# Linear-attention and feed-forward on one core: interleaving the two stages, folding w3 @ w_out, and keeping activations on chip

## The chip, the cores and the metric

One core of one Trainium2 chip runs the whole program. The time is device microseconds of one execution (us). Six parts of the core matter here: PE (TensorE, matrix products and transposes; PEld is its weight load), DVE (VectorE), ACT (ScalarE), POOL (GpSimd, which also issues the converting DMAs of this kernel), SP (SyncE, which issues the other DMAs), and the 16 DMA engines that all queues share. A line number such as L184 is a line of the kernel before.

## The reference, cut to what matters

```python
batch, n_heads, seq, head_dim = (4, 8, 768, 48)        # S = 768, D = 48
for t in range(S):                                      # attention with a decayed state
    kt, vt, rt, wt = (k[:, :, t], v[:, :, t], r[:, :, t], w[:, :, t])
    cur = np.einsum('bhd,bhe->bhde', u[None] * kt, vt)
    y[:, :, t] = np.einsum('bhd,bhde->bhe', rt, state + cur)
    state = wt[:, :, :, None] * state + np.einsum('bhd,bhe->bhde', kt, vt)
x = y.transpose(0, 2, 1, 3).reshape(B * S, H * D)       # 3072 tokens x 384
a = x @ w1                                              # 384 x 1024
b = x @ w2                                              # 384 x 1024
h = a * b @ w3                                          # 1024 x 1024
out = h @ w_out                                         # 1024 x 384, float32
```

There is nothing between `@ w3` and `@ w_out`, so `(a * b) @ (w3 @ w_out)` gives the same output up to rounding.

## The kernel before, in words

The kernel is written in a tile framework: the program names tiles, pools and operations, and the framework puts the instructions of each engine in an order at build time and adds the waits. Each engine then works through its own list in that fixed order. A pool with `bufs=2` gives two buffers in turn; an allocation waits until the oldest buffer is read for the last time.

The work has two stages, one after the other.

Attention treats a batch's 768 steps as 6 chunks of 128. One chunk of one batch is called a unit here; there are 24. Batches go in pairs (`BG = 2`). For each batch r, k and v arrive through POOL's queue (converted to bf16, 0.59 MB each, 6144 rows of 96 bytes) and w through SP's. ACT takes the logarithm of w (L119); per chunk two products with triangular matrices (L129, L132) give running sums, ACT their exponentials, DVE the scaled k and r (L131, L134), and 8 one-column products the decay of the whole chunk (L136). DVE computes the diagonal term for a whole batch at once (L143 to L149). Then each unit runs: 8 transposes of the scaled k and 8 of r, one per head (L166, L170), each set followed by a copy out of PSUM on ACT (L167, L171); 8 products with the state (L178); 8 products between chunk positions (L184), masked on DVE (L186); 8 products with v (L191); the addition of the diagonal (L195); a store of y to DRAM; 8 products that make the state's update (L202), and the update (L206 to L208).

The feed-forward stage reads y back from DRAM with three transposing DMAs (L216) and works on 6 blocks of 512 tokens. Per block: 8 times 3+3 products of 128x128 by 512 columns for a and b (L225, L228), a copy on ACT (L232) and a product on DVE (L233); 64 products of 512 columns with w3 (L239) and 8 copies (L242); 4 times 8 products of 384 columns with w_out (L247), a copy and a store.

The four weight matrices are loaded through POOL's queue, written ahead of r, k and v. Kt_bf, Rt_bf, csp, ktrps, rtrps, Mps, Yps, KVps and y_c in the rows below are tiles of this attention part; a_ps, b_ps, abT, h_ps, hT and o_ps those of the feed-forward.

Of the kernel before, what the change touches and what calls it, by code (L numbers as in the profile page):

```python
# [7 lines left out]
F32 = mybir.dt.float32  # L8
BF = mybir.dt.bfloat16
Alu = mybir.AluOpType  # L10
# [4 lines left out]
def kernel(  # L15
# [12 lines left out]
):  # L28
    nc = tc.nc

    B, H, S, D = r.shape
    C = 128
    NC = S // C
    HC = H * NC
    DM = H * D
    NTOK = B * S
    DFF = moe_w3.shape[0]
    DP = 128

    P = 128  # L40
# [3 lines left out]
    NT = NTOK // TB  # L44

    dram = ctx.enter_context(tc.tile_pool(name="dram", bufs=1, space=bass.MemoryType.DRAM))
    y_dram = dram.tile([NTOK, DM], BF)
    kt_dram = dram.tile([C, HC * DP], BF)
    rt_dram = dram.tile([C, HC * DP], BF)
# [8 lines left out]
    LT_strict = consts.tile([C, C], BF)  # L58
# [4 lines left out]
    mask_tiled = consts.tile([C, H, C], BF)  # L63
    nc.gpsimd.memset(mask_tiled, 1.0)
    nc.gpsimd.affine_select(mask_tiled, mask_tiled, compare_op=Alu.is_gt, fill=0.0,
                            base=0, channel_multiplier=-1, pattern=[[0, H], [1, C]])

    ones_c = consts.tile([C, 1], BF)
    nc.gpsimd.memset(ones_c, 1.0)

    I128 = consts.tile([C, C], BF)
    nc.gpsimd.memset(I128, 0.0)
    nc.gpsimd.affine_select(I128, I128, compare_op=Alu.not_equal, fill=1.0,
                            base=0, channel_multiplier=1, pattern=[[-1, C]])

    u_bc = consts.tile([C, H, D], F32)
    nc.sync.dma_start(u_bc, u.partition_broadcast(C))

    wpool = ctx.enter_context(tc.tile_pool(name="moe_w", bufs=1))
# [3 lines left out]
    wo_bf = wpool.tile([P, FI, DM], BF)  # L83
    nc.gpsimd.dma_start(w1_bf, moe_w1.rearrange("(di dp) f -> dp di f", dp=P))
# [4 lines left out]
    BG = 2  # L89

    with tc.tile_pool(name="attn_io", bufs=2) as sbio, \
         tc.tile_pool(name="attn_sbuf", bufs=BG) as sb, \
         tc.tile_pool(name="attn_sbuf1", bufs=1) as sb1, \
         tc.tile_pool(name="attn_psum", bufs=1, space=bass.MemoryType.PSUM) as ps:

        for bg in range(B // BG):
            st = {}
            for b in range(bg * BG, bg * BG + BG):
                S0_f32 = sb.tile([D, H, D], F32, tag="S0_f")
                S0_bf = sb.tile([D, H, D], BF, tag="S0_b")  # L100
                Kt_bf = sb.tile([C, HC, D], BF, tag="Kt")
                Rt_bf = sb.tile([C, HC, D], BF, tag="Rt")
                Kt4 = Kt_bf.rearrange("t (h c) d -> t h c d", h=H)
                Rt4 = Rt_bf.rearrange("t (h c) d -> t h c d", h=H)

                def rearr(ap):
                    return ap[b].rearrange("h (c t) d -> t (h c) d", t=C)

                r_bf = sbio.tile([C, HC, D], BF, tag="rin")
                k_bf = sbio.tile([C, HC, D], BF, tag="kin")  # L110
                v_bf = sbio.tile([C, HC, D], BF, tag="vin")
                w_f = sbio.tile([C, HC, D], F32, tag="win")
# [12 lines left out]
                r4 = r_bf.rearrange("t (h c) d -> t h c d", h=H)
                pclog_ps = ps.tile([D, HC], F32, tag="pclog", bufs=1)
                for c in range(NC):
                    csp = ps.tile([C, H * D], F32, tag="cs", bufs=1)
                    nc.tensor.matmul(csp, lhsT=LT_incl, rhs=lw4[:, :, c, :], start=True, stop=True)  # L129
                    nc.scalar.activation(NEt, csp, Act.Exp, scale=-1.0)  # L130
                    nc.vector.tensor_mul(Kt4[:, :, c, :], k4[:, :, c, :], NEt)  # L131
                    nc.tensor.matmul(csp, lhsT=LT_strict, rhs=lw4[:, :, c, :], start=True, stop=True)  # L132
                    nc.scalar.activation(Et, csp, Act.Exp)
                    nc.vector.tensor_mul(Rt4[:, :, c, :], r4[:, :, c, :], Et)  # L134
                    for h in range(H):
                        nc.tensor.matmul(pclog_ps[:, h * NC + c:h * NC + c + 1], lhsT=lw4[:, h, c, :],  # L136
                                         rhs=ones_c, start=(c == 0 and h == 0), stop=(c == NC - 1 and h == H - 1))
                pc_all = sb.tile([D, HC], F32, tag="pc_all")
                nc.scalar.activation(pc_all, pclog_ps, Act.Exp)

                uk = sb.tile([C, HC, D], F32, tag="uk")
                d_all = sb.tile([C, HC], F32, tag="d_all")
                nc.vector.tensor_mul(  # L143
                    uk.rearrange("t (h c) d -> t h c d", h=H), k4,
                    u_bc[:, :, None, :].to_broadcast([C, H, NC, D]))
                nc.vector.tensor_mul(uk, uk, r_bf)  # L146
                nc.vector.reduce_sum(d_all, uk, axis=mybir.AxisListType.X)  # L147
                y_diag = sb.tile([C, HC, D], BF, tag="y_diag")
                nc.vector.tensor_mul(y_diag, v_bf, d_all[:, :, None].to_broadcast([C, HC, D]))  # L149

                nc.vector.memset(S0_f32, 0.0)
                nc.vector.memset(S0_bf, 0.0)

                st[b] = dict(S0_f32=S0_f32, S0_bf=S0_bf, Kt4=Kt4, Rt4=Rt4,
                             v4=v_bf.rearrange("t (h c) d -> t h c d", h=H),
                             yd4=y_diag.rearrange("t (h c) d -> t h c d", h=H),
                             pc4=pc_all.rearrange("d (h c) -> d h c", h=H))

            for c in range(NC):
                for b in range(bg * BG, bg * BG + BG):  # L160
                    bs = st[b]
# [12 lines left out]

                    Mbf = sb.tile([C, H, C], BF, tag="M_bf")
                    Yps = ps.tile([C, H * D], F32, tag="Y_ps", bufs=1)
                    for h in range(H):
                        nc.tensor.matmul(Yps[:, h * D:(h + 1) * D], lhsT=RtT[:, h, :],  # L178
                                         rhs=bs["S0_bf"][:, h, :], start=(h == 0), stop=False)
                    for g in range(2):  # L180
                        Mps = ps.tile([C, (H // 2) * C], F32, tag=f"M_ps{g}", bufs=1)
                        for hi in range(H // 2):
                            h = g * (H // 2) + hi
                            nc.tensor.matmul(Mps[:, hi * C:(hi + 1) * C], lhsT=KtT[:, h, :],  # L184
                                             rhs=RtT[:, h, :], start=(hi == 0), stop=(hi == H // 2 - 1))
                        nc.vector.tensor_mul(Mbf[:, g * (H // 2):(g + 1) * (H // 2), :],  # L186
# [23 lines left out]
    with tc.tile_pool(name="moe_sbuf", bufs=2) as msb, \  # L210
# [4 lines left out]
        for di in range(DI):  # L215
            nc.sync.dma_start_transpose(xT[:, di, :], y_dram[:, di * P:(di + 1) * P])  # L216
# [66 lines left out]
```

## Time and profile before

| | us |
|---|---|
| median of 2 runs (419.14 to 419.93) | 419.53 |
| span of the profiled execution, first to last instruction | 417.6 |
| so around the span, by the median | 1.9 |
| PE busy / weight load busy in the span | 315.4 / 177.6 |
| DVE / ACT / POOL busy in the span | 175.6 / 154.9 / 33.4 |

The span is that of one execution under the profiler; the times are of executions without it. Busy time is the sum over instructions of an engine. A PE that is called busy may still be running at half its clock, which the profile gives as the granted clock (1.0 is 2.4 GHz, 0.5 is 1.2 GHz).

### The profile page before, as it was taken

To read this page: it belongs to the slowest core of one execution; us is meant where nothing else is said; L and a number is where in the kernel's file an instruction comes from. 1 tells how busy PE (TensorE), PEld (TensorE's weight loads), DVE (VectorE), ACT (ScalarE), POOL (GpSimd) and SP (SyncE) were. 2 spreads that over 40 slices of the span, in tenths; PEclk is the share of its full clock that TensorE was granted. 3 is DMA by queue.
4 is the path that set the end of the run, shared out by engine and by line. 5 is a ranking of instruction groups with operands and counts; after the bars stand their busy time and mean duration, and the time that the engine had idled before them with its cause. 6 is when DMAs were issued, how large, how long until landed. Compare 5 with 4: busy or idle time off the path is not lost.

```text
span 417.6 us, 5433 instructions
## 1 busy us (share of the span) xinstructions
PE 315.4 (76%) x2256; PEld 177.6 (43%) x2256; DVE 175.6 (42%) x264; ACT 154.9 (37%) x232; POOL 33.4 (8%) x29
## 2 busy tenths in 40 slices
PE   0301034677999747399992699999999999999996
PEld 0201021445777614177771244544544445445443
DVE  1000069795656899975573140330420411402502
ACT  1503033777465336345540133243232332331431
POOL 9100043412000400000000000000000000000000
PEclk9999999985555555655555599999999999999999
DMA  8999999979300980000004700200200201101002
GB/s 157 225 227 215 164 108 129 90 49 111 44 19 26 93 44 2 0 30 21 20 28 98 149 0 2 75 0 2 76 2 0 76 2 38 39 0 57 21 0 75
DMA packets 99400, 26.23 MB, mean 63 GB/s; under 512 B 84144, under 2 KB 97584, under 8 KB 99376
## 3 DMA queue, kind: packets, MB, share of 16 engines
q0 software_dynamic: 76800, 11.54, 40.4%
q1 hardware_dynamic: 22576, 14.36, 13.7%
q8 instruction: 17, 0.28, 0.3%
q14 instruction: 7, 0.06, 0.0%
HBM read 27.98 MB, written 7.08 MB: 84 GB/s over the span
## 4 chain that ended last, share of the span: by engine, by line
PE 63%; DVE 12%; issue 12%; ACT 4%; DMA 4%; POOL 3%; SPq 2%; ACTq 0%; POOLq 0%
PE h_ps L239 20%; PE a_ps L225 8%; PE o_ps L247 7%; PE b_ps L228 7%; PE Mps L184 5%; PE ktrps L166 4%; PE rtrps L170 4%; PE Yps L191 3%; DVE y_diag L149 2%; DMA v_bf<-in_v_dram 2%; DVE d_all L147 2%; DVE uk L146 2%; SPq L216 2%; PE Yps L178 2%; DVE Rt_bf L134 1%
## 5 line engine op out<-in xcount | busy, mean ns | idle before, releaser
L239 PE MATMUL h_ps<-abT,w_bf 128*128 128x512 bf16 x384 | 83.9, 379 | 0.0
L225 PE MATMUL a_ps<-xT,w_bf 128*128 128x512 bf16 x144 | 56.4, 396 | 11.7 <-DMA xT<-y_dram 11.7
L239 PEld LDWEIGHTS <-w_bf 128*128 128x128 bf16 x384 | 37.6, 98 | 45.3
L228 PE MATMUL b_ps<-xT,w_bf 128*128 128x512 bf16 x144 | 56.0, 393 | 0.0
L232 ACT COPY a_sb<-a_ps 128x512 f32<-128x512 f32 x48 | 28.1, 586 | 73.6 <-PE a_ps L225 72.2
L251 DVE COPY o_sb<-o_ps 128x384 f32<-128x384 f32 x24 | 13.4, 557 | 97.5 <-PE o_ps L247 97.5
L233 DVE TENSOR_TENSOR abT<-a_sb,b_ps 128x512 bf16<-128x512 f32 x48 | 33.0, 688 | 47.8 <-ACT a_sb L232 45.9
L242 ACT CAST hT<-h_ps 128x512 bf16<-128x512 f32 x48 | 28.1, 586 | 56.0 <-PE h_ps L239 56.0
L166 PE MATMUL ktrps<-I,Kt_bf 128*48 128x128 bf16 x192 | 30.3, 300 | 23.2 <-DVE Kt_bf L131 22.8
L167 ACT COPY trsb<-ktrps 48x1024 bf16<-48x1024 bf16 x24 | 24.1, 1005 | 38.4 <-PE Yps L178 36.9
L134 DVE TENSOR_TENSOR Rt_bf<-r_bf,Et 128x384 bf16<-128x384 bf16 x24 | 13.1, 546 | 54.9 <-DMA r_bf<-in_r_dram 50.8
L166 PEld LDWEIGHTS <-Kt_bf 128*48 128x48 bf16 x192 | 18.0, 139 | 33.9 <-DVE Kt_bf L131 23.0
L247 PE MATMUL o_ps<-wo_bf,hT 128*128 128x384 bf16 x192 | 32.2, 326 | 0.0
L186 DVE TENSOR_TENSOR Mbf<-Mps,mask_tiled 128x512 bf16<-128x512 f32 x48 | 30.7, 675 | 0.0
L170 PE MATMUL rtrps<-I,Rt_bf 128*48 128x128 bf16 x192 | 28.4, 304 | 2.3 <-ACT trsb L171 1.3
L129 PE MATMUL csp<-lw_bf,LT_incl 128*128 128x384 bf16 x24 | 11.0, 460 | 23.3 <-ACT lw_bf L119 12.8
L184 PE MATMUL Mps<-trsb 48*128 48x128 bf16 x192 | 28.6, 303 | 0.0
L195 DVE TENSOR_TENSOR y_c<-Yps,y_diag 128x384 bf16<-128x384 f32 x24 | 13.4, 557 | 31.2 <-PE Yps L191 31.2
L225 PEld LDWEIGHTS <-w_bf 128*128 128x128 bf16 x144 | 14.6, 101 | 27.6 <-issue 12.1
L171 ACT COPY trsb<-rtrps 48x1024 bf16<-48x1024 bf16 x24 | 24.1, 1005 | 2.1 <-PE rtrps L170 2.1
L130 ACT ACTIVATE NEt<-csp 128x384 f32<-128x384 f32 x24 | 11.7, 489 | 35.0 <-DVE Kt_bf L131 29.0
L247 PEld LDWEIGHTS <-hT 128*128 128x128 bf16 x192 | 18.8, 98 | 13.1
(51 smaller groups left out, 313.8 us busy)
## 6 DMA issues: line engine op xcount, KB each, us to landing
out_dram<-o_sb SPq DMA_DIRECT2D x24, 192.0 KB, 1.9
r_bf<-in_r_dram POOLq DMA_DIRECT2D x4, 576.0 KB, 10.5
k_bf<-in_k_dram POOLq DMA_DIRECT2D x4, 576.0 KB, 8.8
v_bf<-in_v_dram POOLq DMA_DIRECT2D x4, 576.0 KB, 8.5
y_dram<-y_c SPq DMA_DIRECT2D x24, 96.0 KB, 1.6
w_bf<-in_moe_w_dram POOLq DMA_DIRECT2D x1, 2048.0 KB, 26.2
w_bf<-in_moe_w_dram POOLq DMA_DIRECT2D x2, 768.0 KB, 12.3
wo_bf<-in_moe_w_out_dram POOLq DMA_DIRECT2D x1, 768.0 KB, 32.2
```

The lines of the kernel that those rows point to most:

```text
L166: nc.tensor.transpose(ktrps[:, h, :], Kt4[:, h, c, :], I128)
L167: nc.scalar.copy(trsb[:, 0], ktrps)
L170: nc.tensor.transpose(rtrps[:, h, :], Rt4[:, h, c, :], I128)
L184: nc.tensor.matmul(Mps[:, hi * C:(hi + 1) * C], lhsT=KtT[:, h, :], rhs=RtT[:, h, :], start=(hi == 0), stop=(hi == H // 2 - 1))
L186: nc.vector.tensor_mul(Mbf[:, g * (H // 2):(g + 1) * (H // 2), :], Mps.rearrange("s (h t) -> s h t", h=H // 2), mask_tiled[:, :(H // 2), :])
L225: nc.tensor.matmul(a_ps, lhsT=w1_bf[:, di, fi * P:(fi + 1) * P], rhs=xT[:, di, tb * TB:(tb + 1) * TB], start=(di == 0), stop=(di == DI - 1))
L228: nc.tensor.matmul(b_ps, lhsT=w2_bf[:, di, fi * P:(fi + 1) * P], rhs=xT[:, di, tb * TB:(tb + 1) * TB], start=(di == 0), stop=(di == DI - 1))
L232: nc.scalar.copy(a_sb, a_ps)
L233: nc.vector.tensor_mul(abT[:, fi, :], a_sb, b_ps)
L239: nc.tensor.matmul(h_ps, lhsT=w3_bf[:, fi, gi * P:(gi + 1) * P], rhs=abT[:, fi, :], start=(fi == 0), stop=(fi == FI - 1))
L242: nc.scalar.copy(hT[:, gi, :], h_ps)
L247: nc.tensor.matmul(o_ps, lhsT=hT[:, gi, ts * P:(ts + 1) * P], rhs=wo_bf[:, gi, :], start=(gi == 0), stop=(gi == FI - 1))
```

## The change

- w3 @ w_out is computed once on the chip: 64 transposes of 128x128 blocks of w3, then 8 times 8 products of 384 columns into `w34`. Per block the 64 products with w3 are gone; the out products take `abT` and `w34`.
- Two heads share the partitions: scaled k and r lie in tiles padded from 48 to 64 columns a head, so one transpose turns two heads (8 a unit instead of 16, one ACT copy of 128x1024 instead of two of 48x1024). The products between positions take head pairs from partitions 0 to 47 and 64 to 111; the state's update writes two heads to the two halves of PSUM's partitions; the product with the state is one per pair with a block-diagonal state.
- y is transposed on PE (3 a unit) and copied by ACT straight into the feed-forward's input; the DRAM round trip is gone.
- Inputs are loaded per half batch (3 chunks, a group), one DMA per chunk and tensor, the first two groups ahead of the weights. Later groups are written at the first unit of the group two before them.
- The diagonal term is computed per unit, with its three products on POOL; POOL also makes the block-diagonal state (two products a unit).
- The program is written in this order: units 0 to 3, then for each block a quarter of its feed-forward work after each unit of the next block. Blocks 0 to 4 have four units beside them, block 5 none; block 0 also has the w3 @ w_out work.

The core of the new code (the removed lines are those printed above):

```diff
+    ps_ffn = ctx.enter_context(tc.tile_pool(name="ps_ffn", bufs=3, space=bass.MemoryType.PSUM))
+    ps_att = ctx.enter_context(tc.tile_pool(name="ps_att", bufs=2, space=bass.MemoryType.PSUM))
+    ps_m = ctx.enter_context(tc.tile_pool(name="ps_m", bufs=2, space=bass.MemoryType.PSUM))
+    ps_y = ctx.enter_context(tc.tile_pool(name="ps_y", bufs=1, space=bass.MemoryType.PSUM))
...
+    def load_group(b, g):
+        kr_in = inp.tile([C, G, 2, H, D], BF, tag="kr_in")
+        v_in = inp.tile([C, G, H, D], BF, tag="v_in")
+        w_in = inp.tile([C, G, H, D], F32, tag="w_in", bufs=2)
+        for i in range(G):
+            nc.sync.dma_start(w_in[:, i], src(w, b, g)[:, i])
+        for i in range(G):
+            nc.gpsimd.dma_start(kr_in[:, i, 0], src(k, b, g)[:, i])
+            nc.gpsimd.dma_start(kr_in[:, i, 1], src(r, b, g)[:, i])
+        for i in range(G):
+            nc.gpsimd.dma_start(v_in[:, i], src(v, b, g)[:, i])
...
+    def prep_group(b, g):
...
+        for i in range(G):
+            nc.scalar.activation(lw[:, i, :, 0:D], w_in[:, i], Act.Ln)
...
+    def att_a(n):
...
+        for j, (lt, sc) in enumerate(((LT_incl, -1.0), (LT_strict, 1.0))):
+            cs = ps_att.tile([C, H, D], F32, tag="att")
+            nc.tensor.matmul(cs, lhsT=lt, rhs=lw[:, i, :, 0:D], start=True, stop=True)
+            nc.scalar.activation(e_sb[:, j], cs, Act.Exp, scale=sc)
+        krt = kr_st[n % NS]
+        for j in range(2):
+            nc.vector.tensor_mul(krt[:, j, :, 0:D], kr_in[:, i, j], e_sb[:, j])
+        tr = ps_att.tile([C, 2, HP, C], BF, tag="att")
+        for j in range(2):
+            for p in range(HP):
+                nc.tensor.transpose(tr[:, j, p, :],
+                                    krt[:, j, 2 * p:2 * p + 2, :].rearrange("t h d -> t (h d)"), I128)
+        trs = work.tile([C, 2, HP, C], BF, tag="trs")
+        nc.scalar.copy(trs, tr)
+        uk = work.tile([C, H, D], F32, tag="uk")
+        nc.gpsimd.tensor_mul(uk, kr_in[:, i, 0], u_bc)
+        nc.gpsimd.tensor_mul(uk, uk, kr_in[:, i, 1])
+        dsum = work.tile([C, H], F32, tag="dsum")
+        nc.vector.reduce_sum(dsum, uk, axis=mybir.AxisListType.X)
+        yd = work.tile([C, H, D], BF, tag="yd")
+        nc.gpsimd.tensor_mul(yd, v_in[:, i], dsum[:, :, None].to_broadcast([C, H, D]))
...
+    def att_b(n):
...
+        for p in range(HP):
+            for q in range(2):
+                o = q * DP
+                nc.tensor.matmul(mps[q][:, p, :], lhsT=trs[o:o + D, 0, p, :],
+                                 rhs=trs[o:o + D, 1, p, :], start=True, stop=True)
+        for q in range(2):
+            nc.vector.tensor_mul(mbf[:, q], mps[q], mask)
+        if c < NC - 1:
+            kv = ps_att.tile([C, HP, D + 1], F32, tag="att")
+            for p in range(HP):
+                for q in range(2):
+                    nc.tensor.matmul(kv[q * DP:(q + 1) * DP, p, 0:D],
+                                     lhsT=krt[:, 0, 2 * p + q, :], rhs=v_in[:, i, 2 * p + q, :],
+                                     start=True, stop=True)
+                nc.tensor.matmul(kv[:, p, D:D + 1],
+                                 lhsT=lw[:, i, 2 * p:2 * p + 2, :].rearrange("t h d -> t (h d)"),
+                                 rhs=ones_c, start=True, stop=True)
+            nc.scalar.activation(pc[:, :, None], kv[:, :, D:D + 1], Act.Exp)
...
+                nc.vector.tensor_add(ts_, prev[b][0], kv[:, :, 0:D])
...
+            for q in range(2):
+                o = q * DP
+                nc.gpsimd.tensor_mul(s_bd[o:o + DP, :, q * D:(q + 1) * D], ts_[o:o + DP],
+                                     pc[o:o + DP, :, None].to_broadcast([DP, HP, D]))
...
+                nc.vector.tensor_mul(s_f, ts_, pc[:, :, None].to_broadcast([C, HP, D]))
...
+        nc.vector.tensor_add(y_bf.rearrange("t (h e) -> t h e", h=H), y, yd)
+        yt = ps_att.tile([C, DI, C], BF, tag="att")
+        for di in range(DI):
+            nc.tensor.transpose(yt[:, di, :], y_bf[:, di * P:(di + 1) * P], I128)
...
+        nc.scalar.copy(xts[j][:, :, qd * C:(qd + 1) * C], yt)
...
+    def ffn_out(j, t):
+        o_ps = ps_ffn.tile([P, DM], F32, tag="f", name="o_ps")
+        for fi in range(FI):
+            nc.tensor.matmul(o_ps, lhsT=abts[j][:, fi, t * P:(t + 1) * P], rhs=w34[:, fi, :],
+                             start=(fi == 0), stop=(fi == FI - 1))
+        nc.scalar.copy(o_sb, o_ps)
...
+    load_group(0, 0)
...
+    load_group(0, 1)
     nc.gpsimd.dma_start(w1_bf, moe_w1.rearrange("(di dp) f -> dp di f", dp=P))
...
+    def att(n):
+        b, c = divmod(n, NC)
+        if c % G == 0:
+            nxt = b * NG + c // G + 2
+            if nxt < B * NG:
+                load_group(nxt // NG, nxt % NG)
+            prep_group(b, c // G)
+        att_a(n)
+        att_b(n)
...
+    for n in range(UPB):
+        att(n)
+    for j in range(NB):
+        parts = [lambda fi=fi: ffn_ab(j, fi) for fi in range(FI)]
+        if j == 0:
+            parts += fill
+        parts += [lambda t=t: ffn_out(j, t) for t in range(UPB)]
+        units = [n for n in range((j + 1) * UPB, (j + 2) * UPB) if n < NU]
+        k_ = 0
+        for q in range(UPB):
+            if q < len(units):
+                att(units[q])
+            e = len(parts) * (q + 1) // UPB
+            while k_ < e:
+                parts[k_]()
+                k_ += 1
```

`ffn_ab` is the a/b loop of before with both tiles from `ps_ffn`; `fill` is the list of the 8 w3 transpose steps and the 8 product steps into `w34`.

## Rows read from the trace of the kernel before

**Rows 1.** The page: busy us of each engine over the whole span

```profile
PE 315.4 (76%) x2256; PEld 177.6 (43%) x2256; DVE 175.6 (42%) x264; ACT 154.9 (37%) x232; POOL 33.4 (8%) x29
```

**Rows 2.** The page: the span in 40 slices, granted TensorE clock in tenths

```profile
PEclk9999999985555555655555599999999999999999
```

**Rows 3.** Windows: busy us (instructions) of PE, PEld, DVE, ACT, POOL; granted clock, DMA share, GB/s

```profile
100.00:120.00 20.00, 20.00 (x214) 14.77 (x214) 12.11 (x23) 10.74 (x15) 0.00 (x0) 0.50 0.66 56
...
260.00:300.00 40.00, 40.00 (x203) 19.66 (x202) 10.91 (x18) 11.72 (x20) 0.00 (x0) 1.00 0.11 40
```

**Rows 4.** Chain of work that ended last, in order of time: start us, us, what

```profile
109.53 0.43 PE Yps L178 x8
...
111.00 0.54 PE Mps L184 x4
111.54 0.66 PE ktrps L166 x5
...
222.10 0.54 DVE y_c L195
...
231.98 5.45 DMA xT<-y_dram
...
248.32 13.81 PE h_ps L239 x64
262.13 5.20 PE o_ps L247 x32
```

**Rows 5.** Timeline of PE: start us, us, engine, line, operation, tiles, count

```profile
157.18 0.48 PE L132 MATMUL csp<-lw_bf,LT_strict 128*128 128x384 bf16 x1 [1.87 <-ACT NEt L130]
...
165.07 0.85 PE L170 MATMUL rtrps<-I,Rt_bf 128*48 128x128 bf16 x6
...
168.22 0.34 PE L129 MATMUL csp<-lw_bf,LT_incl 128*128 128x384 bf16 x1
```

**Rows 6.** Timeline of the start, all engines

```profile
12.76 0.48 PE L129 MATMUL csp<-lw_bf,LT_incl 128*128 128x384 bf16 x1 [12.76 <-ACT lw_bf L119]
```

**Rows 7.** Windows of the short rise of the clock, columns as in rows 3

```profile
167.00:168.00 1.00, 0.35 (x7) 0.24 (x5) 1.00 (x1) 1.00 (x2) 0.00 (x0) 1.00 0.00 0
...
170.00:171.00 1.00, 0.48 (x1) 0.10 (x1) 1.00 (x2) 0.44 (x2) 0.00 (x0) 0.50 0.00 0
```

**Rows 8.** Instruction groups by line and shape: busy us, mean ns, idle before

```profile
L233 DVE TENSOR_TENSOR abT<-a_sb,b_ps 128x512 bf16<-128x512 f32 x48 | 33.0, 688 | 47.8 <-ACT a_sb L232 45.9 <-PE b_ps L228 1.9
...
L186 DVE TENSOR_TENSOR Mbf<-Mps,mask_tiled 128x512 bf16<-128x512 f32 x48 | 30.7, 675 | 0.0
...
L232 ACT COPY a_sb<-a_ps 128x512 f32<-128x512 f32 x48 | 28.1, 586 | 73.6 <-PE a_ps L225 72.2 <-DVE abT L233 1.4
...
L167 ACT COPY trsb<-ktrps 48x1024 bf16<-48x1024 bf16 x24 | 24.1, 1005 | 38.4 <-PE Yps L178 36.9 <-PE ktrps L166 1.4
...
L131 DVE TENSOR_TENSOR Kt_bf<-k_bf,NEt 128x384 bf16<-128x384 bf16 x24 | 13.1, 547 | 6.7 <-ACT NEt L130 3.9 <-DMA k_bf<-in_k_dram 2.8
...
L130 ACT ACTIVATE NEt<-csp 128x384 f32<-128x384 f32 x24 | 11.7, 489 | 35.0 <-DVE Kt_bf L131 29.0 <-PE csp L129 5.6 <-DVE Rt_bf L134 0.3
...
L147 DVE TENSOR_REDUCE d_all<-uk 128x48 f32<-128x2304 f32 x4 | 10.2, 2542 | 0.0
...
L119 ACT ACT_TABLE_LOAD x4 | 5.1, 1283 | 0.9 <-PEq L267 0.8
...
L65 POOL TENSOR_SCALAR_AFFINE_SELECT mask_tiled<-mask_tiled 128x1024 bf16<-128x1024 bf16 x1 | 1.1, 1081 | 0.0
```

**Rows 9.** Timeline of POOL: the issues of k and v of the first batch

```profile
9.64 2.24 POOL L114 DMA_DIRECT2D k_bf<-in_k_dram  x1
53.20 2.22 POOL L115 DMA_DIRECT2D v_bf<-in_v_dram  x1 [41.32 <-issue]
```

**Rows 10.** Windows of the loads, columns as in rows 3 (last is GB/s)

```profile
24.00:28.00 4.00, 0.00 (x0) 0.00 (x0) 0.00 (x0) 0.00 (x0) 0.00 (x0) 1.00 1.11 226
...
80.00:84.00 4.00, 3.60 (x28) 2.50 (x27) 4.00 (x4) 3.10 (x6) 0.00 (x0) 1.00 2.71 143
```

More of the change, by code (lines that the diff above doesn't have):

```diff
@@ L37 @@
     DFF = moe_w3.shape[0]
-    DP = 128
-    P = 128
+    HP = H // 2
+    DP = 64
     DI = DM // P
@@ new lines, with src @@
+    for t in sb_st:
+        nc.vector.memset(t.rearrange("p h d -> p (h d)").bitcast(F32), 0.0)
+    def src(ap, b, g):
+        return ap[b].rearrange("h (c t) d -> t c h d", t=C)[:, g * G:(g + 1) * G]
+    groups = {}
+    def load_group(b, g):
[9 more added lines that the diff above has]
+            nc.gpsimd.dma_start(v_in[:, i], src(v, b, g)[:, i])
+        groups[b, g] = (kr_in, v_in, w_in)
@@ new lines @@
+    lws = {}
+    def prep_group(b, g):
+        gi = b * NG + g
+        kr_in, v_in, w_in = groups[b, g]
+        lw = lw_st[gi % NS]
+        for i in range(G):
+            nc.scalar.activation(lw[:, i, :, 0:D], w_in[:, i], Act.Ln)
+        lws[b, g] = lw
+    state = {}
+    def att_a(n):
+        b, c = divmod(n, NC)
+        g, i = divmod(c, G)
+        kr_in, v_in, _ = groups[b, g]
+        lw = lws[b, g]
+        e_sb = work.tile([C, 2, H, D], F32, tag="e_sb")
+        for j, (lt, sc) in enumerate(((LT_incl, -1.0), (LT_strict, 1.0))):
[19 more added lines that the diff above has]
+        nc.gpsimd.tensor_mul(yd, v_in[:, i], dsum[:, :, None].to_broadcast([C, H, D]))
+        state[n] = (krt, trs, yd)
@@ new lines, with ffn_ab @@
+    xts = {}
+    abts = {}
+    out3 = out.rearrange("(n t) o -> n t o", t=P)
+    def ffn_ab(j, fi):
+        if fi == 0:
+            abts[j] = big.tile([P, FI, TB], BF, tag="abT", name=f"abT{j}")
+        x = xts[j]
+        a_ps = ps_ffn.tile([P, TB], F32, tag="f", name="a_ps")
+        for di in range(DI):
+            nc.tensor.matmul(a_ps, lhsT=w1_bf[:, di, fi * P:(fi + 1) * P], rhs=x[:, di, :],
+                             start=(di == 0), stop=(di == DI - 1))
+        b_ps = ps_ffn.tile([P, TB], F32, tag="f", name="b_ps")
+        for di in range(DI):
+            nc.tensor.matmul(b_ps, lhsT=w2_bf[:, di, fi * P:(fi + 1) * P], rhs=x[:, di, :],
+                             start=(di == 0), stop=(di == DI - 1))
+        a_sb = work.tile([P, TB], F32, tag="a_sb")
+        nc.scalar.copy(a_sb, a_ps)
+        nc.vector.tensor_mul(abts[j][:, fi, :], a_sb, b_ps)
@@ new lines, in w34_mul @@
+    def w34_mul(fi):
+        pm = ps_ffn.tile([P, DM], F32, tag="f", name="pm")
+        for gi in range(FI):
+            nc.tensor.matmul(pm, lhsT=w3T[:, gi, fi * P:(fi + 1) * P], rhs=wo_bf[:, gi, :],
+                             start=(gi == 0), stop=(gi == FI - 1))
+        nc.scalar.copy(w34[:, fi, :], pm)
+    load_group(0, 0)
+    nc.sync.dma_start(u_bc, u.partition_broadcast(C))
+    nc.gpsimd.memset(I128, 0.0)
+    nc.gpsimd.affine_select(I128, I128, compare_op=Alu.not_equal, fill=1.0,
+                            base=0, channel_multiplier=1, pattern=[[-1, C]])
```

244 lines of the change are left out of this document (77 added, 167 removed).

## The prediction

> **What bounds the kernel now.** I read the engines' sums first: PE is busy 315.4 of 417.6 us, twice any other [rows 1]. The slices then show that this is not one state: the granted clock is full from the feed-forward stage on and half in most of attention [rows 2]. The windows give the two levels: attention from 100 to 120 us has PE busy all 20 us at 0.50 (1.2 GHz), the feed-forward from 260 to 300 all 40 us at 1.00 (2.4 GHz), DVE and ACT at most 60% in both [rows 3]. So from 100 us on PE is the bound whenever work is there. Two stretches are not PE's: the start, where the loads decide, since POOL's issue of v stands 41.32 us behind that of k [rows 9]; and the handover, where the last y is added at 222.6 and the transposing reads land at 231.98 + 5.45 = 237.4 us [rows 4]: 15 us with hardly any work on PE. The 1.0 of the first slices is not to be believed as speed: a 384-column product at 12.76 us took 0.48 us [rows 6], as at the granted 0.50 at 157 us, while the one at 168 us, granted 1.00, took 0.34 [rows 5].
>
> **The change part by part.**
>
> *w3 @ w_out once.* Removed are 384 products of 512 columns: 64 took 13.81 us, 215.8 ns each [rows 4], so 82.9 us of PE at full clock, all on the path. Their 48 copies on ACT lay beside them and count nothing. Added on PE: 64 products of 384 columns at 5.20/32 = 162.5 ns [rows 4] = 10.4 us, and 64 transposes. Five transposes took 0.66 us at the half clock, 132 ns each [rows 4]; at full clock I take half, 66 ns, so 4.2 us. Net saving 68 us. What stays: 288 products x 215.8 ns = 62.1 us and 192 x 162.5 ns = 31.2 us. The feed-forward needs 62.1 + 31.2 + 14.6 = 107.9 us at full clock, twice that at half.
>
> *Attention on PE, per unit.* Before, at half clock: 16 transposes x 132 + 8 products of Mps x 135 (four in 0.54) + 24 of 48 columns x 54 (eight in 0.43) = 4.5 us [rows 4]. After: 11 transposes, 8 Mps, 20 narrow ones, 4 of 96 columns at 108 ns, and the two 384-column sums, which were in a stretch of their own (0.48 us each [rows 5]): 1.45 + 1.08 + 1.08 + 0.43 + 0.96 = 5.0 us at half clock. At full clock the wide ones halve (the sums 0.34 each by the row) and the narrow ones lie between half and unchanged: 2.7 to 3.25 us; I take 3.0, since a short product has a part that no clock shortens. No row has two Mps products side by side on the two halves of the rows; if pairs overlap entirely, 0.27 us less (2.4 at the lowest), if not at all, nothing is lost, and a handover between array shapes could add to it: four Mps of 128 columns at 1.2 GHz would be 0.43 us and took 0.54, so 0.11 us for each turn, and with about 8 turns a unit 0.9 us at the half clock, 0.45 at full. PE in all: 107.9 + 24 x 3.0 = 180 us at full clock, 335 at half.
>
> *The DRAM round trip.* The 15 us go. The 3 transposes a unit are counted above; the copy is one of 384 columns on ACT (0.49 us, as L130 [rows 8]), beside other work.
>
> *DVE and ACT, whole kernel.* A unit costs DVE 2 x 0.547 + 0.42 (a sixth of 2.54) + 2 x 0.675 + 2 x 0.3 + 0.55 = 4.0 us [rows 8]; with 48 x 0.688 for abT and 8 copies of w3's transposes (about 1.1 us each, by L167's width): 96 + 33 + 9 = 138 us. ACT: 2 x 0.489 + 1.0 + 0.49 + 0.2 = 2.7 us a unit, 64 in all, the logarithms 12, a_sb 28, 32 copies of 384 columns 16, and table loads. There was one load each way per use of the logarithm (four of them on L119 [rows 8], as many elsewhere); with 8 groups that is 16 x 1.28 = 21 us, and 62 if each of the 24 calls is parted from the next. ACT 141 to 182 us. Beside 180 on PE both are hidden unless the upper end holds.
>
> *POOL.* Five multiplications a unit move there. No row has a two-input operation on POOL. The nearest has one input (1.081 us for 1024 elements [rows 8], so 0.41 us for 384). Three operations of 384 and two of 192 elements cost 1.6 us a unit at that rate, 4.9 if both inputs and the output each take such a pass. I take two passes, one an input: 3.3 us, 79 in all. The Trainium skill ("GPSIMD Engine Reference", section "Performance versus the Vector engine") says that elementwise work with two inputs is about half as fast there as on VectorE, which speaks against this move; by its 2.6 cycles an element at 1.2 GHz, an estimate from that page, 384 elements take 0.83 us and a unit 3.3; no run here shows it. The 72 DMA issues cost between 0.37 us (a sixth of 2.2 [rows 9], by their size) and 0.9 each: 27 to 65 us. POOL ends between 65 and 183 us, taken as 120.
>
> *The loads.* Windows show 226 GB/s with the weights and 143 with the 96-byte rows of r and k alone [rows 10]. A group's k, r, v (0.88 MB) is 6.2 us, its w (0.59 MB) 2.6, w1 and w2 (1.57 MB) 6.9, w3 and w_out (2.88 MB) 12.8. From 2 us: group 0 in by 11, group 1 by 20, with w of groups 2 and 3 running ahead on SP w1 and w2 by 32, the rest by 45, group 2 by 51 us. One unit's chain (sums 0.48, exponentials 2 x 0.49, products 2 x 0.55, transposes 1.05, copy 1.0, Mps 1.1, masks 1.35, v 0.5, addition 0.55, transposes 0.4, copy 0.5) is 9 us, so unit 3 is through by about 30 and the feed-forward can start at 30 to 36; I take 34. By then units 0 to 5 have been worked on. *The wait that this adds:* POOL's list has group 0, the masks, group 1, the weights and group 2 ahead of unit 0's multiplications. The old kernel held a third load of 6144 rows back until the first of three had landed [rows 9], so POOL should stand until group 0 and half of group 1 are in, about 15 us, with the diagonal terms queued behind and y waiting for them. Four units at 3.3 us then end near 29 us: just covered by the 34.
>
> *Overlap.* In the chain transposes of the next unit stand between the two halves of Mps [rows 4], so the instruction order mixes units and PE had no gap at 100 us [rows 3]. I let it mix blocks and units as well.
>
> *The sum.* From 34 us PE has 107.9 + 18 x 3.0 = 162 us. It was full in rows 3, but units 6 and 7 wait for group 2 until 51 us, the turns of shape are not in the 3.0, and DVE and ACT are 65% full: I take 92%, 176 us. Then 0.5 for the last copy and 2 for the store: 212.5 us of span, against 417.6. With the 1.9 us around it (median less span) **214 us**.
>
> **The rivals.**
>
> *POOL or ACT is late (235).* If the queue holds POOL until the weights are in (45 us), y of units 0 to 3 comes at about 55 and everything moves by 20 us: 235. The same time comes if ACT's 182 us holds. For it: the 41 us in rows 9. Against it: the inputs now stand ahead of the weights.
>
> *The clock (275 to 340).* Attention at full density stayed at 0.50 for 100 to 120 us [rows 3]; at 166 us it rose for some 3 us after a dense run of transposes and sums, and fell when PE was a third to three quarters busy [rows 5, 7]. If a mixed stretch does not hold full clock, 34 + 2 x 107.9 + 18 x 5.0 = 340 us; with half of it slow, 275. Against it: more than half of the mixed work is what held 1.00 in rows 3. The Trainium skill ("TensorE: Matmul & The Clock Gate", section "Part 4: PE-mode transpose") says that transposes do not count as work for the clock; the rise at 166 us came amid transposes, but with sums among them, so the trace does not settle it, and by that rule this rival is somewhat likelier.
>
> *Serial units (slower, 437).* If the build order leaves PE waiting inside each unit, nothing of the feed-forward fills it: 24 chains of 9 us are 216, and with such gaps the clock stays at half, so another 216 for the feed-forward, and 5 for the start: 437. It decides only if both hold; with full clock in the bursts it is 335.
>
> **How the numbers follow.** The forecast (196 to 235) has 0.70, the late queue (235 to 260) 0.10, the clock (260 to 345) 0.16, serial units 0.04. The lower end is 2.4 us a unit and a full PE: 34 + 107.9 + 43 + 4.4 = 189, which leaves no slack at all; I put 195. The upper end takes in the case of half the stretch slow, 276. About 2% is what a measurement here tells from no change. Faster by over 2%: 0.95; within 2%: 0.02, as no case ends there; slower: 0.03.
>
> **What would show it.** First block product near 34 us; PE busy over 90% from there to the end; granted clock 1.00 there; 16 table loads; about 15.6 us of feed-forward alone at the end; no line with w3's 512-column products. It is wrong if the clock row shows long stretches of 5, if the releaser ahead of PE's idle time is POOL or a load after 60 us, or if one unit takes over 7 us of any engine.

## The result, and the profile after

The changed kernel takes 325.58 us (323.39 to 327.78, two runs) against 419.53: ratio 0.776, 95% interval 0.7635 to 0.7885. It is faster, as forecast, but by 94 us where 205 were forecast, and 325.6 lies far above the range of 195 to 276.

The page after: busy time by engine, the clock in 40 slices, and the shares of the chain that ended last.

```profile
PE 210.5 (65%) x1624; PEld 112.5 (35%) x1624; DVE 138.3 (42%) x246; ACT 154.6 (47%) x254; POOL 156.8 (48%) x200
...
PEclk9999999999999999789999965999679995999599
...
PE 41%; DMA 19%; ACT 15%; DVE 9%; POOL 8%; issue 6%; ACTq 0%; DVEq 0%; POOLq 0%
```

PE fell from 315 us [rows 1] to 210, the clock is up in nearly all of the span where it was half for most of attention [rows 2]. Yet no engine is over 65%: PE does not bound the kernel as a whole any more. In the chain that ended last it has only 41%. So something makes the engines wait, and the timelines show that there are two such things.

The first is the start. Timeline of POOL after, 27 to 62 us (start us, us, engine, line, operation; in brackets the idle time and what ended it):

```profile
27.77 0.74 POOL L284 DMA_DIRECT2D w_bf<-in_moe_w_dram  x1 [1.10 <-DMA kr_in<-in_r_dram]
...
31.76 0.90 POOL L286 DMA_DIRECT2D w_bf<-in_moe_w_dram  x1 [1.27 <-DMA kr_in<-in_r_dram]
33.77 0.88 POOL L287 DMA_DIRECT2D wo_bf<-in_moe_w_out_dram  x1 [1.12 <-DMA kr_in<-in_k_dram]
...
41.72 0.87 POOL L111 DMA_DIRECT2D kr_in<-in_k_dram  x1 [2.37 <-DMA w_bf<-in_moe_w_dram]
...
55.33 0.88 POOL L114 DMA_DIRECT2D v_in<-in_v_dram  x1 [9.02 <-DMA w_bf<-in_moe_w_dram]
59.19 1.75 POOL L114 DMA_DIRECT2D v_in<-in_v_dram  x2 [2.99 <-DMA wo_bf<-in_moe_w_out_dram]
60.95 0.93 POOL L152 TENSOR_TENSOR uk<-kr_in,u_bc 128x384 f32<-128x384 bf16 x1
```

Each issue waits until the transfer issued eight places earlier on this queue has landed: the load at 41.72 us for w1 (issued at 27.77, landed after 13.7), the one at 55.33 for w3, the one at 59.19 for w_out. All of group 2 stands ahead of the first multiplication of unit 0 in POOL's list, so this comes at 60.95 us, when every weight is on the chip. The addition of y waits for it on DVE, and PE for the addition. PE's timeline after:

```profile
26.97 0.46 PE L218 MATMUL y<-v_in,mbf 128*128 128x48 bf16 x7 [0.38 <-DVE mbf L177]
67.20 0.50 PE L226 MATMUL yt<-I,y_bf 128*128 128x128 bf16 x3 [39.77 <-DVE y_bf L223]
67.50 0.53 PE L138 MATMUL cs<-lw,LT_incl 128*128 128x384 bf16 x1
68.27 0.48 PE L138 MATMUL cs<-lw,LT_strict 128*128 128x384 bf16 x1 [0.25 <-ACT xT L230]
...
79.31 0.50 PE L226 MATMUL yt<-I,y_bf 128*128 128x128 bf16 x3 [0.65 <-DVE y_bf L223]
...
89.82 0.50 PE L226 MATMUL yt<-I,y_bf 128*128 128x128 bf16 x3 [0.65 <-DVE y_bf L223]
...
99.84 0.50 PE L226 MATMUL yt<-I,y_bf 128*128 128x128 bf16 x3 [0.65 <-DVE y_bf L223]
...
101.18 1.49 PE L242 MATMUL a_ps<-xT,w_bf 128*128 128x512 bf16 x3
```

All of unit 0 but the diagonal term was done at 27.4 us; then PE stands still for 39.77 us. The second thing is in the same rows: the first sum of unit 1 (cs) comes right after the last transposes of unit 0 (yt), the second after the copy of these (xT). So a unit starts when the one before it ends, 10 to 12 us apart, and unit 3 is through at 100 us, not at 30. The feed-forward starts at 101.2 us.

It goes on like this beside the feed-forward. ACT after, 165 to 176 us, one unit:

```profile
165.05 0.48 ACT L230 COPY xT<-yt 128x384 bf16<-128x384 bf16 x1
165.55 1.28 ACT L139 ACT_TABLE_LOAD   x1
166.84 0.87 ACT L139 ACTIVATE e_sb<-cs 128x384 f32<-128x384 f32 x2
...
168.88 1.01 ACT L149 COPY trs<-tr 128x1024 bf16<-128x1024 bf16 x1 [0.69 <-PE tr L146]
...
171.17 1.28 ACT L124 ACT_TABLE_LOAD   x1
172.47 0.52 ACT L124 ACTIVATE lw<-w_in 128x384 bf16<-128x384 f32 x1
...
174.84 0.48 ACT L230 COPY xT<-yt 128x384 bf16<-128x384 bf16 x1
```

From one copy of a transposed y to the next 9.8 us pass, and every step of the unit lies between. From the first to the last of the 24 units the mean distance is 10.3 us. The feed-forward fills PE's gaps, but not all: windows of 40 us after (columns as in rows 3) show 30 to 35 of 40 us busy, at a granted clock of 0.83 to 0.96.

```profile
100.00:140.00 40.00, 35.38 (x275) 19.17 (x274) 22.63 (x38) 23.19 (x36) 20.16 (x25) 0.96 0.52 38
...
180.00:220.00 40.00, 30.18 (x232) 15.11 (x229) 21.08 (x37) 26.91 (x43) 21.98 (x27) 0.83 0.49 43
```

**Theory A:** two losses, a late start (POOL's list) and a chain of units. **Rivals:** PE with its clock is the bound anyway (B); the DMA engines, not the order of the list, set the start (D); the table loads make the chain.

### The profile page after: what moved, and what is told of

Same layout as the page of the kernel before. It is cut to its first block, busy times and chain, and to the rows that moved or that the text cites. A ratio compares the mean times of both kernels' runs of the same rounds, so it can differ in the third digit from the quotient of the medians.

```text
span 326.0 us, 4347 instructions
## 1 busy us (share of the span) xinstructions
PE 210.5 (65%) x1624; PEld 112.5 (35%) x1624; DVE 138.3 (42%) x246; ACT 154.6 (47%) x254; POOL 156.8 (48%) x200
## 4 chain that ended last, share of the span: by engine, by line
PE 41%; DMA 19%; ACT 15%; DVE 9%; POOL 8%; issue 6%; ACTq 0%; DVEq 0%; POOLq 0%
PE a_ps L242 9%; DMA wo_bf<-in_moe_w_out_dram 8%; PE b_ps L246 7%; PE o_ps L255 5%; DMA kr_in<-in_k_dram 5%; ACT L139 5%; PE tr L146 4%; DMA kr_in<-in_r_dram 3%; PE pm L270 3%; PE kv L183 3%; DVE krt L142 3%; DVE mbf L177 3%; DMA out_dram<-o_sb 2%; PE kv L186 2%; ACT e_sb L139 2%
## 5 line engine op out<-in xcount | busy, mean ns | idle before, releaser
L142 DVE TENSOR_TENSOR krt<-kr_in,e_sb 128x384 bf16<-128x384 bf16 x48 | 29.0, 631 | 40.6 <-ACT e_sb L139 40.4
L146 PE MATMUL tr<-I,krt 128*128 128x128 bf16 x192 | 22.4, 252 | 30.9 <-DVE krt L142 30.6
L149 ACT COPY trs<-tr 128x1024 bf16<-128x1024 bf16 x24 | 24.3, 1012 | 28.6 <-PE tr L146 27.0
L177 DVE TENSOR_TENSOR mbf<-m,mask 128x512 bf16<-128x512 f32 x48 | 30.8, 684 | 15.8 <-PE m L174 15.8
L255 PE MATMUL o_ps<-w,abT 128*128 128x384 bf16 x192 | 36.4, 325 | 0.0
L111 POOL DMA_DIRECT2D kr_in<-in_k_dram x24 | 22.1, 922 | 20.3 <-DVE krt L142 9.3
L152 POOL TENSOR_TENSOR uk<-kr_in,u_bc 128x384 f32<-128x384 bf16 x24 | 23.6, 987 | 14.1 <-DVE dsum L155 14.1
L112 POOL DMA_DIRECT2D kr_in<-in_r_dram x24 | 21.6, 900 | 5.5 <-DMA w_bf<-in_moe_w_dram 2.8
L153 POOL TENSOR_TENSOR uk<-uk,kr_in 128x384 f32<-128x384 f32 x24 | 22.5, 938 | 1.6
L139 ACT ACTIVATE e_sb<-cs 128x384 f32<-128x384 f32 x48 | 22.0, 492 | 0.6 <-PE cs L138 0.3
```

What stands on the lines that cost most here:

```text
L139: nc.scalar.activation(e_sb[:, j], cs, Act.Exp, scale=sc)
L142: nc.vector.tensor_mul(krt[:, j, :, 0:D], kr_in[:, i, j], e_sb[:, j])
L146: nc.tensor.transpose(tr[:, j, p, :], krt[:, j, 2 * p:2 * p + 2, :].rearrange("t h d -> t (h d)"), I128)
L149: nc.scalar.copy(trs, tr)
L152: nc.gpsimd.tensor_mul(uk, kr_in[:, i, 0], u_bc)
L177: nc.vector.tensor_mul(mbf[:, q], mps[q], mask)
```

## The experiments

In the table each kernel's span is split at the first product of the feed-forward (a_ps, read from PE's timeline): what lies before it is the start, the rest runs to the end. The medians come from two runs each, the ratios are to the kernel before, and start and rest come from one execution, whose time lies up to 2.2 us from the median.

| kernel | median us | ratio, 95% interval | start, us | rest, us |
|---|---|---|---|---|
| the change | 325.6 | 0.776 [0.764, 0.789] | 101.2 | 224.8 |
| e1_dve | 293.1 | 0.700 [0.688, 0.711] | 71.5 | 221.7 |
| e2_late | 315.2 | 0.753 [0.748, 0.758] | 89.8 | 224.0 |
| e3_ytbank | 302.4 | 0.722 [0.717, 0.727] | 93.7 | 207.0 |
| e4_ahead | 297.8 | 0.711 [0.704, 0.718] | 95.9 | 199.3 |
| e5_ln1 | 317.2 | 0.757 [0.745, 0.770] | 99.4 | 214.0 |
| e6_lncopy | 310.1 | 0.741 [0.734, 0.747] | 99.3 | 210.2 |
| e9_both | 302.2 | 0.722 [0.718, 0.726] | 92.4 | 208.1 |
| e10_dve_ahead | 250.2 | 0.598 [0.594, 0.602] | 57.1 | 191.0 |
| c1_all | 241.5 | 0.577 [0.574, 0.579] | 53.6 | 186.4 |
| c2_worder | 237.6 | 0.568 [0.560, 0.575] | 54.2 | 180.4 |
| c3_ytbank | 248.9 | 0.595 [0.585, 0.604] | 54.2 | 191.4 |

**The multiplications back on DVE (e1_dve).**

```diff
-        nc.gpsimd.tensor_mul(uk, kr_in[:, i, 0], u_bc)
-        nc.gpsimd.tensor_mul(uk, uk, kr_in[:, i, 1])
+        nc.vector.tensor_mul(uk, kr_in[:, i, 0], u_bc)
+        nc.vector.tensor_mul(uk, uk, kr_in[:, i, 1])
...
-        nc.gpsimd.tensor_mul(yd, v_in[:, i], dsum[:, :, None].to_broadcast([C, H, D]))
+        nc.vector.tensor_mul(yd, v_in[:, i], dsum[:, :, None].to_broadcast([C, H, D]))
...
-                nc.gpsimd.tensor_mul(s_bd[o:o + DP, :, q * D:(q + 1) * D], ts_[o:o + DP],
+                nc.vector.tensor_mul(s_bd[o:o + DP, :, q * D:(q + 1) * D], ts_[o:o + DP],
```

> One part undone: the five multiplications of a unit go from POOL to DVE, everything else as in the changed kernel (325.6 us). Theory A (late start: the first unit's y waits at 66.6 us for a diagonal term that stands on POOL behind the issue of every load up to group 2, until 60.95 us; after that units follow each other as a chain of about 10.2 us each): the first y comes near 28 us, the whole chain moves up by about 38 us, 285 to 292 us; POOL's list then holds only DMA issues. Rival B (PE with the clock sets the end, the start only fills time that PE has to spend later anyway): less than 15 us, 310 us or more. Rival C (DVE becomes the bound with 2.5 us more a unit): 320 us or more.

293.1 us: 32.5 less, a little short of theory A's range and far from B and C. The first transposed y comes at 28.5 us. Almost all of the gain is in the start (101 to 72 us); the rest does not move, and the mean distance of the units stays at 10.5 us. Beside the 5.5 us missing to the 38 stands one new wait of 10.5 us on DVE (its timeline in this kernel):

```profile
51.75 1.03 DVE L142 TENSOR_TENSOR krt<-kr_in,e_sb 128x384 bf16<-128x384 bf16 x2 [2.32 <-ACT e_sb L139]
63.30 0.56 DVE L152 TENSOR_TENSOR uk<-kr_in,u_bc 128x384 f32<-128x384 bf16 x1 [10.52 <-DMA kr_in<-in_k_dram]
...
66.96 1.28 DVE L177 TENSOR_TENSOR mbf<-m,mask 128x512 bf16<-128x512 f32 x2
```

A multiplication that reads k stands in DVE's list ahead of unit 3's masks, and its k comes only with group 2, behind the weights. The same fault, on another engine: a list in fixed order with an early place for late data.

**Group 2 loaded later (e2_late).**

```diff
         if c % G == 0:
-            nxt = b * NG + c // G + 2
-            if nxt < B * NG:
-                load_group(nxt // NG, nxt % NG)
             prep_group(b, c // G)
         att_a(n)
         att_b(n)
+        if c % G == G - 1:
+            nxt = b * NG + c // G + 2
+            if nxt < B * NG:
+                load_group(nxt // NG, nxt % NG)
```

> The multiplications stay on POOL, but the loads of the group after next are written after the last unit of a group instead of ahead of its first. Theory A: POOL then comes to the first multiplication after the issue of the last weight matrix (34.7 us instead of 60.95), the first y moves from 66.6 to about 40 us, and the time falls by about 26 us, to 296 to 303, unless a group then comes too late for its first unit. Rival B (PE sets the end): 315 us or more. Rival D (the DMA engines themselves, not the order of POOL's list, set the start): within 3 us of 325.6.

315.2 us: 10.4 less, neither the 26 of theory A nor the nothing of D. POOL did come to the first multiplication at 34.9 us and the first y at 41. But the build order put the group's loads between the multiplications of the next units. POOL's timeline here:

```profile
34.03 0.87 POOL L287 DMA_DIRECT2D wo_bf<-in_moe_w_out_dram  x1 [1.26 <-DMA kr_in<-in_k_dram]
34.92 0.93 POOL L152 TENSOR_TENSOR uk<-kr_in,u_bc 128x384 f32<-128x384 bf16 x1
...
55.77 0.87 POOL L114 DMA_DIRECT2D v_in<-in_v_dram  x1 [6.33 <-DMA w_bf<-in_moe_w_dram]
59.59 0.87 POOL L114 DMA_DIRECT2D v_in<-in_v_dram  x1 [2.95 <-DMA wo_bf<-in_moe_w_out_dram]
```

The wait for the weights thus moved from in front of unit 0 to in front of unit 2, whose y comes 21.7 us after that of unit 1. It is the order of the list; the data were there.

**A PSUM bank for the transposed y (e3_ytbank), the order of halves (e4_ahead), both (e9_both).**

```diff
-    ps_ffn = ctx.enter_context(tc.tile_pool(name="ps_ffn", bufs=3, space=bass.MemoryType.PSUM))
+    ps_ffn = ctx.enter_context(tc.tile_pool(name="ps_ffn", bufs=2, space=bass.MemoryType.PSUM))
+    ps_t = ctx.enter_context(tc.tile_pool(name="ps_t", bufs=1, space=bass.MemoryType.PSUM))
...
-        yt = ps_att.tile([C, DI, C], BF, tag="att")
+        yt = ps_t.tile([C, DI, C], BF, tag="yt")
```

```diff
-    def att(n):
+    def pre(n):
         b, c = divmod(n, NC)
...
         att_a(n)
-        att_b(n)
+
+    def att(n):
+        if n + 1 < NU:
+            pre(n + 1)
+        att_b(n)
+
+    pre(0)
```

> Only the PSUM pools: the transposed y gets a bank of its own (the feed-forward pool goes from 3 to 2 banks), so the two sums of the next unit need not wait for the copy of this unit's transposed y. Theory A1 (units form a chain because five tiles a unit share two PSUM banks, and the second sum of a unit waits for the copy of the last unit's transposed y): units overlap, the distance of one unit's transposed y to the next falls from 10.2 to 7 to 8 us, and the time to 270 to 290. Rival A2 (the build order itself keeps units apart, banks or not, as each unit is written whole before the next): distance stays near 10, time within 6 us of 325.6. Rival B (PE is the bound from 105 us on): no change, or slower through the feed-forward's lost bank.

> Only the order in which the program is written: the first half of unit n+1 (logarithm, sums, exponentials, transposes) is written ahead of the second half of unit n; pools as in the changed kernel. Theory A1 or A2 (a chain of units of 10.2 us): halves of neighbouring units overlap, the distance falls to 6.5 to 8 us and the time to 265 to 285, with the start still at 67 us. Rival B (PE bound): PE stays 85% busy after 105 us and the time within 10 us of 325.6.

> On the changed kernel, both ways to open the chain of units at once: the own PSUM bank for the transposed y (alone 302.4 us) and the order with the next unit's first half ahead (alone 297.8). If both cure the same wait (the next unit's sums stand behind this unit's last copy), the second adds little: 290 to 300 us. If they cure two waits, their gains of 23 and 28 us add: 274 us. POOL's list is as in the changed kernel, so the first transposed y stays at 66 to 73 us either way.

302.4, 297.8 and 302.2 us. Each alone brings the mean distance of units from 10.3 to about 9 us and takes 18 to 26 us off the rest; this refutes B, since PE has the same work. The gains are smaller than expected in both, and the pair lies above the range given for it. A2 is out at its price, but not the order as such: the framework built another list with the bank. PE's timeline of e3 has the first sum of unit 1 ahead of unit 0's products with v, where the change has it behind unit 0's transposed y (67.50 us):

```profile
24.26 0.50 PE L139 MATMUL cs<-lw,LT_incl 128*128 128x384 bf16 x1
...
26.59 0.22 PE L219 MATMUL y<-v_in,mbf 128*128 128x48 bf16 x1 [0.52 <-DVE mbf L178]
```

So in e3 the free tile and the earlier place come together, and no run parts them. Together the two edits give no more than the bank alone. That fits one wait, the second sum's wait for a PSUM tile that the transposed y holds, but does not show it: both kernels with the bank leave the feed-forward two banks, and there b_ps waits for abT, 8.0 us in e3 and 7.9 in e9 (95 to 300 us), a wait that the change and e4 do not have. The start falls by only 5 to 9 us in all three, as POOL still comes late. The mean granted clock goes from 0.926 to 0.983 (e3) and 0.965 (e4), so a part of the gain may be the clock's.

**The table loads (e5_ln1, e6_lncopy).**

```diff
-        for i in range(G):
-            nc.scalar.activation(lw[:, i, :, 0:D], w_in[:, i], Act.Ln)
+        nc.scalar.activation(lw.rearrange("p g h d -> p (g h) d")[:, :, 0:D],
+                             w_in.rearrange("p g h d -> p (g h) d"), Act.Ln)
```

```diff
-            nc.scalar.activation(lw[:, i, :, 0:D], w_in[:, i], Act.Ln)
+            nc.scalar.activation(lw[:, i, :, 0:D], w_in[:, i], Act.Copy, scale=-0.1)
```

> The logarithm of a group is one instruction instead of three; all else as in the changed kernel. There the tables are loaded 34 times (17 for the logarithm, 17 for the exponential) at 1.283 us, since the three logarithms of a group are taken one by one between the units. Expected 16 to 18 loads. If the load ahead of the exponentials lies in the chain of a unit (theory A1), 16 units lose one of 1.28 us: 20 us less, 303 to 308 us. If the loads lie beside other work, within 6 us of 325.6.

> The logarithm is replaced by a copy scaled by -0.1, which leaves it out: the output is another one, the work is the same but for the tables, which are then loaded once. If a table load lies in the chain of each unit: 24 x 1.28 = 31 us less, 292 to 298 us, the distance of one unit's transposed y to the next 1.3 us shorter. If not: within 6 us of 325.6.

317.2 and 310.1 us. The change has 34 loads (17 for the logarithm, 17 for the exponentials, one of these at L190), e5 has 14, fewer than expected, and e6 one. Both times lie between the two cases given. The rows of the change:

```profile
L124 ACT ACT_TABLE_LOAD x17 | 21.8, 1283 | 4.5 <-DMA w_in<-in_w_dram 4.1
...
L139 ACT ACT_TABLE_LOAD x16 | 20.5, 1283 | 0.3
```

Of 33 loads (42 us on ACT) 15.4 us show in the time. So they are a part of the loss, though not the 31 us expected: 17 loads stand ahead of exponentials, for 24 units, and other work may use part of that time, which no run shows. The interval of e5 alone (0.745 to 0.770) overlaps that of the change (0.764 to 0.789), so its 8.4 us are not settled by that pair.

**The fold alone, on the kernel before (e7_fold).** The 64 products with w3 are gone from the loop, the transposes and products into w34 stand ahead of it, and the out products take abT and w34:

```diff
-            hT = msb.tile([P, FI, TB], BF, tag="hT")
...
-                    nc.tensor.matmul(o_ps, lhsT=hT[:, gi, ts * P:(ts + 1) * P],
-                                     rhs=wo_bf[:, gi, :],
+                    nc.tensor.matmul(o_ps, lhsT=abT[:, gi, ts * P:(ts + 1) * P],
+                                     rhs=w34[:, gi, :],
```

> The kernel before with one part of the change alone: w3 @ w_out is computed once, the 384 products of 512 columns go; attention and the order of the stages are those of before. The prediction's term: 82.9 us off the path, 14.6 added on PE (to be seen where they land): 419.5 - 68 = 351 us. If the added products are placed into PE's idle start, 338 us; if the feed-forward then waits for ACT or DVE instead of PE, 360 us or more.

338.2 us, ratio 0.808 [0.804, 0.811]: 80.5 us less, nearly the whole 82.9. The chain of waits shows where the added work went:

```profile
221.78 0.54 DVE y_c L198
222.37 2.82 PE pt L224 x24
...
228.73 10.56 PE pm L229 x64
...
249.65 5.26 PE o_ps L253 x32
```

It fills the gap between the stages that was left empty in the old kernel [rows 4]. The sum expected 338 for an idle place at the start; the place was another. What follows weighs more: this one part gives 81 of the 94 us. All the rest of the change, which was to bring twice as much, brought 12.6.

**Putting the edits together (e10_dve_ahead, c1_all, c2_worder, c3_ytbank).** e10 has the edits of e1 and e4; c1 that of e5 as well; c3 is c1 with the own bank of e3; c2 is c1 with group 2 issued ahead of w3 and w_out:

```diff
+    load_group(1, 0)
     nc.gpsimd.dma_start(w3_bf, moe_w3.rearrange("(fi fp) g -> fp fi g", fp=P))
     nc.gpsimd.dma_start(wo_bf, moe_w_out.rearrange("(gi gp) o -> gp gi o", gp=P))
...
-            if nxt < B * NG:
+            if 2 < nxt < B * NG:
```

> Three edits together: the five multiplications on DVE, the first half of the next unit written ahead of the second half of this one, one logarithm a group. If start and chain are separate losses they add up: 325.6 - 33 (multiplications on DVE, measured) - 28 (order, measured) = 265, with fewer table loads 250 to 262. If PE is the bound once the chain is open, its 187 busy us after the start at about 60 us give 250 and no less. If DVE, with some 2.5 us more a unit, takes over: 275 or more.

> The multiplications on DVE and the order with the next unit's first half ahead, but the three logarithms of a group as in the changed kernel. If start (33 us alone) and chain (28 alone) are separate losses: 262 to 268 us, and the one logarithm a group is worth the rest down to 241.5. If the logarithm is worth only what it was alone (8 us): 249 us, and opening the chain is then worth more once the start is early.

> The three edits (241.5 us together) and group 2 issued ahead of w3 and w_out instead of behind them. If what is left of the start is a wait for group 2 behind the weights (its last loads are issued at 56 to 64 us): 230 to 238 us. If PE, busy 82% of 240 us, is the bound with what it has to do by then: 239 to 243. Slower if the products into w34 then wait for w3.

> The three edits (241.5 us together) and the own PSUM bank for the transposed y. If units still wait for each other: 225 to 235 us. If PE is the bound: 238 to 246, slower where the feed-forward misses its third bank.

250.2, 241.5, 237.6 and 248.9 us. c1 lies below and c3 above all that was expected of them; e10 lies beside its second case and c2 in its first. Start and chain do more than add up: 32.5 + 27.8 would be 60, e10 gains 75. Of the surplus 9 us are in the start, where the two take 44 us off and 30 + 5 alone, and 5 in the rest (34, against 3 + 26). In e1, with the first y early, units 1 and 2 still followed at 10 us each and unit 3's masks stood behind group 2; with both edits the distances are 7, 9 and 8 us. c2 is below c1 by 4 us, but their intervals overlap, so that is not settled. The own bank loses 7 us in c3: there the chain is open already, and b_ps waits for abT nine times, 2.8 us in all (60 to 240 us), which it does not in c1. That points to the feed-forward's missing third bank; the rest of the 7 us is not accounted for. The window of c2 (columns as in rows 3) shows PE as the bound again, as it was in the old kernel, at full clock now; in the next three windows of 40 us PE is busy 34.9, 38.6 and 38.6 us:

```profile
60.00:100.00 40.00, 37.91 (x325) 23.09 (x327) 32.73 (x66) 19.23 (x37) 15.76 (x18) 1.00 1.55 130
```

c2 has the lowest median here: 43% below the kernel before and 27% below the change.

## Why the prediction was wrong, point by point

- **The step that failed first: "Overlap".** "I let it mix blocks and units as well" rested on two rows of the old kernel, where each kind of tile had PSUM of its own. The change gives five tiles of a unit two banks; the prediction does not follow the waits that this makes between units. The rest of the run, forecast at 178.5 us from 34 to 212.5, was 224.8. With the chain opened by order (e4) it is 199.3, with the multiplications off POOL too 191.0, with fewer table loads 186.4, with group 2 earlier 180.4: the forecast is nearly reached when PE is let work. The terms for PE were thus about right (180 us forecast, 189.5 busy in c2).
- **The step that failed second: the wait on POOL, "just covered by the 34".** I took rows 9 as a limit of rows in flight and had POOL free at 15 us; it was free at 60.95, since each issue waits for the transfer eight before it and the weights are among these. I named the queue and what stands behind it, but not its length in transfers: 9 a group where the old kernel had 3 a batch. The hold in rows 9 was another one: v was the seventh transfer on its queue and waited for r, issued at 7.45 us and landed 45.4 us later. What sets either limit is not shown. The start was 101 us instead of 34; putting the multiplications on DVE alone gives back 30, with the chain open too 44. The remaining 20 of the 67 are in c2 still. The traces show two things that go into them: the last r of the first group lands at 17.5 us in the change, where the whole group was to be in by 11, and units pass at 6 to 9 us in c2 where I let them pass at 3 to 4.
- **The fold:** right in mechanism, its size off by 12 us in the old kernel (68 forecast, 80.5 measured), as the added work shares the gap of the round trip, which I counted as a gain of its own. Within the new structure it was not measured alone.
- **Attention on PE:** 3.0 us a unit at full clock was near, by errors that cancel. From start to next start, one unit of the change at full clock (168 to 176 us) takes 2.95 us: less than forecast for the products of head pairs, which run side by side (0.33 us for eight, below), and for the two sums (0.16 each, where 0.34 was in the sum); more for eight transposes (0.80, where 0.53 was in the sum) and for the twelve narrow products of the state's update (0.94, where 54 ns each was the upper end).
- **DVE, ACT, POOL:** DVE 138.3 us was forecast as 138. ACT was forecast as 141 to 182 and is 154.6, with 34 table loads instead of 16. POOL was forecast as 120 (65 to 183) and is 156.8; a multiplication of 384 elements took 0.86 to 0.99 us, with 0.82 in the sum. Its sum was not what hurt, its order was.
- **The rivals:** "POOL is late" was the true one for the start, at a price of 20 us instead of 33 (e1) to 48 (from e4 to e10). "Serial units" was true in its first half (units in a chain) and false in its second (the feed-forward does fill PE between their steps); its price with the full clock in the bursts, 335, is 329 by its own terms (216 + 108 + 5). So the truth lay between two rivals that I had priced one by one, and never together. The clock's price, 275 to 340, holds the measured 325.6 by luck: its condition, half of the stretch or all of it at the half clock, did not come. The granted clock was 0.926 on the whole, and 1.00 in c2.
- **Sign and chance:** faster by over 2% held.

## What to carry to other kernels

Before an overlap is counted, write down for one unit which buffer each step takes and which step of the unit before frees it; if the last step of one unit frees what the first of the next needs, the units cost at least their chain, whatever the engines' sums say. An engine that issues transfers and computes has one list: work behind an issue waits for everything that issue waits for, so count the transfers ahead of it, not only their bytes. And split a large change before pricing it: here one part alone on the old kernel gave 81 of 94 us.

## What the runs showed of the hardware that was not expected

Products of head pairs on the two halves of the partitions run side by side: eight took 0.53 us to the next product, as long as four of the old kernel at the half clock [rows 4]. The pace was that of the half clock here too, though the record says 1.00: four transposes just before (72.21 us) took 0.54 us to the next product. At 170.68 us, granted 1.00 as well, the eight took 0.33 us; one by one they would be 0.43, an estimate from the 215.8 ns of 512 columns [rows 4]. The narrow products alternate with a one-column product over the full width, and two with one of these took 0.30 us, 100 ns each instead of 54. PE's timeline after:

```profile
74.23 0.25 PE L183 MATMUL kv<-v_in,krt 128*64 128x48 bf16 x2
74.42 0.18 PE L186 MATMUL kv<-ones_c,lw 128*128 128x1 bf16 x1
74.53 0.25 PE L183 MATMUL kv<-v_in,krt 128*64 128x48 bf16 x2
...
75.14 0.61 PE L174 MATMUL m<-trs 48*128 48x128 bf16 x8
75.67 0.50 PE L213 MATMUL y<-sbd,trs 128*128 128x96 bf16 x4
...
170.68 0.40 PE L174 MATMUL m<-trs 48*128 48x128 bf16 x8
171.01 0.34 PE L213 MATMUL y<-sbd,trs 128*128 128x96 bf16 x4
```

DVE is slower beside multiplications on POOL. Of the 16 products of 192 elements (s_f) three took 0.65 to 1.08 us in the change; with POOL's multiplications gone (e1, e10, c1) none is over 0.36. The scaled k and r (krt) went from 0.63 to 0.55 us in the mean, which is the old kernel's value [rows 8]. Products with one input in PSUM hardly changed (abT 685 ns in the change, 682 in e1). DVE after:

```profile
75.49 0.34 DVE L195 TENSOR_TENSOR ts__312<-s_f,kv 128x192 f32<-128x192 f32 x1
75.87 1.08 DVE L203 TENSOR_TENSOR s_f<-ts__312,pc 128x192 f32<-128x192 f32 x1
```

By the Trainium skill ("GPSIMD Engine Reference", section "Specifications") VectorE and GpSimd share their SBUF interfaces, with contention where a VectorE instruction has two SBUF inputs; s_f and krt have two, so the rows agree.
